# Attention beside an MLP on one core: the output's scale made in the head, other lengths for the pieces of other work, transposes ahead of the lengths

## The chip, the core and the metric

The kernel runs on one core of a Trainium2 chip. Its time is the device time of an execution in microseconds; three runs are given, and their median is the kernel's time. A profiled execution of its own gives the trace.

## What is computed

The input x has 2048 rows of 640. It is normalised by row, and the result xn goes two ways: attention with 32 heads of 20, and an MLP that normalises once more. Both are added to x.

```
xn = layernorm(x)
qkv = (xn @ wqkv) -> q, k, v of 32 heads, 2048 x 20 each
p = softmax(q @ k.T * 20**-0.5)          # 2048 x 2048, 32 times
A = concat(p @ v) @ wo
h = gelu(layernorm(xn) @ w1 + b1)        # 2048 x 1536, tanh form
B = h @ w2 + b2
out = x + A + B
```

## The kernel before

**Number formats.** Most products are of float32 values that are split into a high and a low float16 part, and three matmuls (high by high, high by low, low by high) stand for one. A weight is scaled by a power of two before it is split. `pow2` (line 107) makes that scale from sums of squares: a tiny matmul (tile mxp) adds 128 partitions' sums by a matrix of ones, and VectorE reduces it and takes the exponent with a few one-column operations (`lo_`, `hi_`, `s_` tiles). `scale_of` (456) calls it for q, k, v, w1, w2 and wo, under the tags "q", "k", "v", "1", "2" and "o". The tile of mxp comes from the pool psM (one buffer) for the tags "k" and "o", otherwise from psS (three buffers, which the scores share).

**The head** (up to 183 us). Four chunks of 512 rows of x are normalised (`norm_a`, `norm_b`, `norm_c`), transposed (for chunk 1 by TensorE in `transp`, with `transp_out` to evict), and multiplied with wqkv (`qk`, tiles qkp; `qk_out` evicts to qkhl by ScalarE L367 and VectorE L368; `vproj` and `vproj_all` make the values). `lengths` adds squares of q and k by head on TensorE (tile norms). Five steps a chunk are written out as strings at line 643, one letter per action: "4" and "6" are lengths, "!", "@" and "#" the three transposes of chunk 1, "t" an eviction of one of them, "c" is norm_c, "o" is qk_out, "q" and "y" ask for a piece of w1 and of w2, "w" makes the scale of v, and "s" takes one step of `weights()`, a generator that squares, scales and splits w1 and that collects the squares of wo.

**The loop** (183 to 1265 us) has 64 passes: 16 pairs of heads, two halves of the queries, two quarters in each half. A pass works on 512 queries of two heads in 16 units of 128 keys. For a unit TensorE makes the scores (L786, tile s in one of psS's three buffers), ScalarE the exponential (L788, tile p, seven buffers), and TensorE the product with the values (L818, tile o). In half of the units p is a sum of its upper bfloat16 half and a float16 rest `low`, which VectorE subtracts (L800, four buffers); the products of four units are issued together.

Beside this run the pieces of other work on TensorE: the first layer of the MLP (tile pu, 30 matmuls of 256 columns for one evicted tile), the second layer (py, 36 of 320), the values of the later heads (pz, 15 of 480) and at last the output product (z, 15 of 320). All four share psM's single buffer. A finished pu tile starts a `gelu`, a chain of eight operations on VectorE (L1010 to L1025) with a tanh on ScalarE between (L1021).

The order is by a table. PLAN has seven rows of steps for a pass: "s" is a unit's scores and exponential, "v4" the products of the four oldest units, "l4" the low part of unit 4, "e" the eviction of the pass before, "m" a piece of other work, and "t" or "r" a tick. A tick moves every side job by one step: a gelu, an eviction, the loads of the next heads, the finishing of results, the split of w2 and wo. With "r" a gelu's tanh waits one tick more. RATE gives the three "m" of a pass their lengths in us of TensorE: `other` saves them up as credit and cuts a tile's matmuls at the nearest places. Where a new gelu starts while the one before is unfinished, the rest of the old one is issued first (line 1085).

In pass 4 the generator `values` (1147) takes one "m" for the scales: it makes f2, fills a second ones tile (`wones`, GpSimd), calls `scale_of("o")`, makes fo from it, and starts the split of w2 (`second_split`).

After the loop 27 of the 32 output tiles are left.

Of the kernel before, what the change touches and what calls it, by code (L numbers as in the profile page):

```python
# [9 lines left out]
F32 = mybir.dt.float32  # L10
# [4 lines left out]
ALU = mybir.AluOpType  # L15
# [3 lines left out]
P = 128  # L19
# [13 lines left out]
KROW = 32768.0  # L33
GRP = 4
CHUNK = 2.1
RATE = (1.75, 1.95, 1.9)
PLAN = ('s s t v4 e l0', 's s t s l1 r m r r l4', 's s v4 l5', 's s r t m', 's s s l8 r v4', 's l9 r l12 s l13 m', 's r s v4')
UNITS = (3, 3, 3, 3, 2, 2)
ENDS = tuple(sum(UNITS[: i + 1]) for i in range(len(UNITS)))
TAIL = 12  # L40
# [3 lines left out]
MC = 256  # L44
# [4 lines left out]
def mha_mlp_kernel(tc, x, wqkv, wo, w1, b1, w2, b2, out):  # L49
# [4 lines left out]
    with (  # L54
# [53 lines left out]
        def pow2(acc, tag, total=None):  # L108

            lo = keep.tile([P, 1], F32, name=f"lo_{tag}")  # L110
            hi = keep.tile([P, 1], F32, name=f"hi_{tag}")
            if total is None:
                if tag in "ko":
                    pt = psM.tile([P, 512], F32, tag="m", name="mxp")
                else:
                    pt = psS.tile([P, 2, 512], F32, tag="s", name="mxp")[:, 0, :]
                n = acc.shape[1]
                nc.tensor.matmul(pt[:, :n], ones_of[0], acc, start=True, stop=True)
                nc.vector.tensor_reduce(lo, pt[:, :n], AX.X, ALU.add)  # L119
                total = lo  # L120
            nc.vector.tensor_scalar(lo, total, 2.0**-100, 2.0**120, ALU.max, ALU.min)

            nc.vector.tensor_scalar(lo.bitcast(I32), lo.bitcast(I32), 0x7F000000, 1,
                                    ALU.bitwise_and, ALU.logical_shift_right)
            if tag == "q":

                scales[tag] = keep.tile([P, 1], F32, name=f"s_{tag}")
                nc.vector.tensor_scalar(hi.bitcast(I32), lo.bitcast(I32), 0x3F800000, None, ALU.bitwise_xor)
                nc.vector.tensor_scalar(scales[tag], hi, 2.0**76, None, ALU.mult)
                return lo, hi  # L130
            whole(lo, hi)
            return lo, hi
# [46 lines left out]
        with tc.tile_pool(name="pa", bufs=2) as pa, tc.tile_pool(name="pa1", bufs=1) as pa1, tc.manual_schedule():  # L179
# [278 lines left out]
            def scale_of(tag, total=None):  # L458
                pw[tag] = pow2(accs[tag], tag, total)
                if tag not in scales:  # L460
                    scales[tag] = keep.tile([P, 1], F32, name=f"s_{tag}")
                    nc.vector.tensor_scalar(scales[tag], pw[tag][1], 4096.0, None, ALU.mult)
                if tag == "k":
                    back(tag)
# [37 lines left out]
            def weights():  # L502

                for k in range(KD):
                    if k == 0:
                        accs["1"] = sm.tile([P, 8], F32, tag="acc1", name="acc1", bufs=1)[:, :KD]
                    nc.scalar.activation(junk[:, :F], w1t[:, k, :], AF.Square, accum_out=accs["1"][:, k : k + 1])
                    yield
                scale_of("1")
                yield  # L510
                factors()
                yield

                accs["o"] = sm.tile([P, 8], F32, tag="acco", name="acco", bufs=1)[:, :KD]
                came = []
                for n in range(3 * KD):
                    k, q = divmod(n, 3)
                    if q == 2:
                        nc.scalar.activation(junk[:, :D], came[-1], AF.Square, accum_out=accs["o"][:, k : k + 1])
                    split(pa, w1t[:, k, q * 512 : (q + 1) * 512], w1v[:, k, q, 0], w1v[:, k, q, 1], scales["1"], 512)  # L520
                    if q == 0:
                        came.append(pa.tile([P, D], F32, tag="wtmp", name="wos"))
                        nc.gpsimd.dma_start(came[-1], wo[k * P : (k + 1) * P, :])
                    yield

            def second():

# [92 lines left out]
            for c in range(4):  # L620
                nxt = c + 1 if c < 3 else None
                for tt in range(5):
                    if c == 0 and tt == 1:
                        norm_b2(0)
                        norm_c(0)

                        nc.scalar.activation(junk[:, :1], ones[:, :1], AF.Exp)
                        ps = qk(0, 1, lambda: scale_of("k"))
                        hl = qk_out(0, 0, first)
                        split_qkv("q", c0=4 * P)  # L630
                        split_qkv("k")
                    else:
                        ps = qk(c, tt)
                    if c == 0:
                        if tt == 0:
                            split_qkv("q", c0=2 * P, c1=4 * P)
                            sums("k", [stage["k"][:, 0:3], stage["k"][:, 3:]])
                            first = ps
                            continue
                        elif tt == 1:  # L640
                            qk_sq(0, 0, hl)
                            pts = []
                    for step in (('', 'qvo', 'ao', 'bo', '4q!y@c#otyxttSywz'), ('zos', 'qa6yqoPsbiqs', 'jkso', 'lcsV4o', 'sxoy'), ('ssoa6bzijP', 'yo', 'zs4ossc', 'klozV', 'uozs'), ('so', 'os6', 'oszs', 'ssosPsVfze4', 'o'))[c][tt]:
                        if step == "a":
                            norm_a(nxt)
                        elif step == "b":
                            norm_b(nxt)
                        elif step == "c":
                            norm_c(nxt)
                        elif step in "!@#":  # L650
                            transp(1, 2 * "!@#".index(step), pts)
                        elif step == "t":
                            transp_out(*pts.pop(0))
                        elif step in "46":
                            lengths(int(step))
                        elif step == "x":
                            load_x(c + 2)
                        elif step == "s":
                            some(1)
                        elif step == "q":  # L660
                            ask(1)
                        elif step == "z":
                            next(slices2, None)
                        elif step == "y":
                            next(asked2, None)
                        elif step == "v":
                            sums("v", [stage["v"][:, 0:3], stage["v"][:, 3:]])
                        elif step == "w":
                            scale_of("v")
                            split_qkv("v")  # L670
                        elif step == "u":
                            for s in range(2):
                                nc.sync.dma_start(vwscr[:, :, s], wv[:, :, 2, s, VC:])
                        elif step == "f":
                            factors_out()
                        elif step == "S":
                            qk_sq(0, 4, hl)
                        elif step == "o":
                            hl = qk_out(c, tt, ps)
                        elif step == "P":  # L680
                            vp = vproj(c - 1)
                        elif step == "V":
                            head_values(c - 1, vp)
                        elif step == "e":
                            early = [load_features(mc) for mc in range(2)]
                        else:
                            turn(nxt, "ijkl".index(step))
# [13 lines left out]
            some(99)  # L701
            for _ in slices2:
                pass


        with ExitStack() as scope:
# [438 lines left out]
            def values(hv, feats):  # L1145

                step = (D - VC) / 2400
                for kb in range(NKB - 4):
                    c, j = divmod(kb, MC // P)
                    if kb == 2:  # L1150
                        yield 1, 0.2
                        nc.vector.tensor_scalar(f2, ulo, 2.0**-14, pw["2"][0], ALU.mult, ALU.mult)
                        nc.vector.tensor_scalar(f2, f2, 2.0**-13, None, ALU.mult)
                        ones_of[0] = m1.tile([P, 2 * MC], F32, tag="w", name="wones")[:, :P]
                        nc.gpsimd.memset(ones_of[0], 1.0)
                        scale_of("o")
                        nc.vector.tensor_scalar(fo, pw["v"][0], 2.0**-22, pw["o"][0], ALU.mult, ALU.mult)
                        late.append(second_split())
                        patient.append(late[0])
                        yield 0.2  # L1160
                    yield 3 * KD, 3 * KD * step
                    ps = psM.tile([P, 512], F32, tag="m", name="pz")
                    n = 0
# [313 lines left out]
```

## Time and profile before

| | us |
|---|---|
| three runs | 1326.13, 1329.0, 1329.7 |
| median | 1329.0 |
| the profiled execution | 1328.16 |
| its span, first to last instruction | 1326.3 |
| TensorE (PE) busy | 1314.0 |
| ScalarE (ACT) busy | 1116.3 |
| VectorE (DVE) busy | 1065.3 |
| granted TensorE clock | 0.999 |

The difference of 1.9 us between the execution and its span lies outside the recorded instructions. PE counts as busy while a matmul is issued or under way, so its busy share is not its peak. In the chain of waits and in the timeline a row begins with the start and the length in us; `x15` is a count of merged instructions, and a bracket tells how long the engine idled before and what ended it. In rows of groups there stand, behind the bar, the busy us and the mean ns of one, and behind the second bar the idle time before them.

### The profile page before, as it was taken

How to read it: one execution, taken by the hardware profiler on the slowest of the kernel's cores; microseconds unless marked ns; L12 is line 12 of the kernel's file. 1: busy time of each engine (PE TensorE's matmuls, PEld its weight loads, DVE VectorE, ACT ScalarE, POOL GpSimd, SP SyncE). 2: the span in 40 equal slices, each digit the busy share in tenths (PEclk: the TensorE clock that was granted, in tenths of full speed). 3: DMA queues.
4: the chain of work that ended last, by engine and by line, in shares of the span. 5: the costliest groups of instructions: out<-in, count | busy, mean ns of one | idle time of the engine just before them, and what ended most of it. 6: DMA issues, size and time to landing. Idle time of an engine off the chain costs nothing.

```text
span 1326.3 us, 29078 instructions
## 1 busy us (share of the span) xinstructions
PE 1314.0 (99%) x11636; PEld 604.2 (46%) x11636; DVE 1065.3 (80%) x1450; ACT 1116.3 (84%) x1306; POOL 36.1 (3%) x85
## 2 busy tenths in 40 slices
PE   9999999999999999999999999999999999999998
PEld 6454564333344444444444444444444444443466
DVE  7667569898699887889988798987889898988642
ACT  7745369999999999999999999999999999989900
POOL 2000000000000000000000000000000000000000
PEclk9999999999999999999999999999999999999999
DMA  8697531121233321142312034222124332253266
GB/s 308 215 276 214 190 103 35 39 63 53 77 82 99 86 57 33 44 120 64 97 47 68 17 88 123 69 55 58 50 59 117 92 87 70 71 158 100 87 216 192
DMA packets 108166, 135.28 MB, mean 102 GB/s; under 512 B 24308, under 2 KB 74376, under 8 KB 107900
## 3 DMA queue, kind: packets, MB, share of 16 engines
q1 hardware_dynamic: 104588, 125.99, 31.9%
q0 software_dynamic: 2816, 6.90, 2.7%
q8 instruction: 92, 1.51, 0.5%
q10 hardware_dynamic: 624, 0.51, 0.1%
q14 instruction: 46, 0.38, 0.1%
HBM read 86.64 MB, written 43.74 MB: 98 GB/s over the span
## 4 chain that ended last, share of the span: by engine, by line
PE 72%; DVE 15%; ACT 5%; DMA 4%; issue 2%; SPq 1%; ACTq 0%; DVEq 0%; POOLq 0%
PE o L818 23%; PE s L786 15%; PE pu L1079 10%; PE py L1114 8%; DVE low L800 6%; PE qkp L352 6%; PE z L1264 5%; PE pz L1166 3%; ACT p L788 2%; PE vp L425 1%; DMA xb<-in_B_b_dram 1%; DVE w L1014 1%; DVE u L1012 1%; DVE u L1010 1%; DVE w L1016 1%
## 5 line engine op out<-in xcount | busy, mean ns | idle before, releaser
L788 ACT ACTIVATE p<-s 128x1024 f32<-128x1024 f32 x1024 | 968.7, 1057 | 56.2 <-PE s L786 53.9
L800 DVE TENSOR_TENSOR low<-p 128x1024 f16<-128x1024 f32 x512 | 605.7, 1219 | 72.8 <-ACT p L788 71.4
L818 PE MATMUL o<-p,vfull 128*32 128x512 bf16 (+1 forms) x4096 | 384.1, 493 | 0.0
L786 PE MATMUL s<-qs,ks 61*128 61x512 f16 x2048 | 303.5, 381 | 3.0 <-ACT p L788 2.1
L786 PEld LDWEIGHTS <-ks 61*128 61x128 f16 x2048 | 75.7, 94 | 234.8 <-issue 215.8
L1114 PE MATMUL py<-w2t,hT 128*128 128x320 f16 x1152 | 171.5, 300 | 0.9 <-DVE xb L1041 0.9
L1079 PE MATMUL pu<-xm,w1t 128*128 128x256 f16 x1440 | 171.4, 273 | 0.1
L1079 PEld LDWEIGHTS <-w1t 128*128 128x128 f16 x1440 | 134.3, 98 | 43.9 <-issue 29.3
L818 PEld LDWEIGHTS <-vfull 128*32 128x32 f16 x3072 | 61.1, 95 | 183.3 <-issue 182.7
L1114 PEld LDWEIGHTS <-hT 128*128 128x128 f16 x1152 | 105.6, 98 | 71.2 <-issue 33.9
L352 PE MATMUL qkp<-xnt,wv 128*128 128x512 f16 x600 | 131.4, 379 | 1.6 <-DVE lo L119 0.8
L818 PE MATMUL o<-low,vfull 128*32 128x512 f16 x1024 | 101.5, 378 | 0.1
L352 PEld LDWEIGHTS <-wv 128*128 128x128 f16 x600 | 58.0, 98 | 70.9 <-issue 1.7
L818 PEld LDWEIGHTS o<-p,vfull 128*32 128x32 f32 x2048 | 61.8, 108 | 58.3
L1264 PE MATMUL z<-w1t,ot 128*128 128x320 f16 x480 | 66.7, 299 | 0.0
L1010 DVE TENSOR_TENSOR u<-pu,r2f 128x512 f32<-128x512 f32 x48 | 33.1, 689 | 36.2 <-PE pu L1079 36.0
L1264 PEld LDWEIGHTS <-ot 128*128 128x128 f16 x480 | 46.3, 98 | 21.0 <-issue 3.3
L367 ACT ACTIVATE qkhl<-qkp,qks 128x1024 f16<-128x1024 f32 (+1 forms) x24 | 23.2, 965 | 37.2 <-PE qkp L352 15.3
L1221 DVE SCALAR_TENSOR_TENSOR acc<-z,sc,acc 128x320 f32<-128x320 f32 x32 | 17.6, 550 | 42.0 <-PE z L1264 41.7
L368 DVE SCALAR_TENSOR_TENSOR qkhl<-qkp,qks,qkhl 128x1024 f16<-128x1024 f32 (+1 forms) x24 | 26.5, 1105 | 26.1 <-ACT qkhl L367 26.0
L843 ACT ACTIVATE ev<-o 128x512 f32<-128x512 f32 x64 | 39.5, 617 | 3.0 <-PE o L818 2.8
L1104 POOL DMA_DIRECT2D xb<-in_B_b_dram x16 | 13.7, 857 | 953.7 <-DMA xb<-in_A_x_dram 352.4
(206 smaller groups left out, 735.2 us busy)
## 6 DMA issues: line engine op xcount, KB each, us to landing
qkscr<-qkhl SPq DMA_DIRECT2D x40, 256.0 KB
opart<-ev SPq DMA_DIRECT2D x124, 80.0 KB
ks<-qkscr SPq DMA_DIRECT2D x120, 80.0 KB
xm<-xscr SPq DMA_DIRECT2D x13, 640.0 KB
qs<-qkscr SPq DMA_DIRECT2D x192, 40.0 KB
oa<-opart SPq DMA_DIRECT2D x32, 240.0 KB
xt<-in_A_x_dram SPq DMA_DIRECT2D x16, 320.0 KB
xscr<-xnt SPq DMA_DIRECT2D x4, 1280.0 KB
```

Source lines behind the costliest of these rows:

```text
L352: nc.tensor.matmul(ps[:, i, :], wv[:, k, q, a, mm * P : (mm + 1) * P], xnts[c][:, k, b, :], start=(k + n == 0), stop=(k == KD - 1 and n == 2))
L368: nc.vector.scalar_tensor_tensor(hl[:, 1, i0:i1], ps[:, i0:i1], a, hl[:, 0, i0:i1], ALU.mult, ALU.subtract)
L786: nc.tensor.matmul(ps[:, a, :], ks[64 * a : 64 * a + 61, kb * P : (kb + 1) * P], qs[64 * a : 64 * a + 61, cc * 512 : (cc + 1) * 512], star ...
L788: nc.scalar.activation(pt, ps, AF.Exp, scale=QS)
L800: nc.vector.tensor_sub(low, pt, upper(pt))
L818: nc.tensor.matmul(pv.o[32 * q : 32 * q + 32, :], src[:, v0 - PAD * (1 - q % 2) :][:, :32], t, start=q not in pv.begun, stop=last, skip_gr ...
L843: nc.scalar.activation(evs[g, hf][:, cc], o, AF.Copy)
L1010: nc.vector.tensor_mul(u, ps, r2f[:, None, :].to_broadcast([P, 2, MC]))
L1079: nc.tensor.matmul(ps[:, i], w1v[:, k, (f + i) // 4, a, fo_ : fo_ + P], xnt[:, k, b, :], start=(n == 0), stop=(n == 3 * KD - 1))
L1114: nc.tensor.matmul(ps[:, :320], hTs[mc][:, f, a, j * P : (j + 1) * P], w2v[:, f, b, hf * 320 : (hf + 1) * 320], start=(n == 0), stop=(n == ...
L1166: nc.tensor.matmul(ps[:, : D - VC], feats[c][:, k, a, j * P : (j + 1) * P], hv[:, k, b, :], start=(n == 0), stop=(n == 3 * KD - 1))
L1264: nc.tensor.matmul(ps[:, :320], ot[:, k, a, j * P : (j + 1) * P], wov[:, k, b, h * 320 : (h + 1) * 320], start=(n == 0), stop=(n == 3 * KD ...
```

## The change

Five edits. RATE and PLAN get other numbers and another order. The tag "1" joins those whose mxp tile is of psM. The scale of wo and the factor fo are made as the last step of `weights()`, in the head, and f2 at the head's end; the step in `values` goes, and with it the second ones tile. In the head's strings chunk 0's last step has the transposes first and the lengths behind them, and norm_c behind two evictions.

```
-RATE = (1.75, 1.95, 1.9)
-PLAN = ('s s t v4 e l0', 's s t s l1 r m r r l4', 's s v4 l5', 's s r t m', 's s s l8 r v4', 's l9 r l12 s l13 m', 's r s v4')
+RATE = (2.0, 1.4, 2.2)
+PLAN = ('s s t v4 l0 e', 's s l1 t s r m', 's s t v4', 's s l4 r l5 l8 m', 's s t l9 s r v4', 's l12 s m l13', 's r s v4')
...
-                if tag in "ko":
+                if tag in 'ko1':
...
+                scale_of("o")
+                nc.vector.tensor_scalar(fo, pw["v"][0], 2.0**-22, pw["o"][0], ALU.mult, ALU.mult)
...
-                    for step in (('', 'qvo', 'ao', 'bo', '4q!y@c#otyxttSywz'), ...
+                    for step in (('', 'qvo', 'ao', 'bo', '!y@#4qottctyxSywz'), ...
...
+            nc.vector.tensor_scalar(f2, ulo, 2.0**-14, pw["2"][0], ALU.mult, ALU.mult)
+            nc.vector.tensor_scalar(f2, f2, 2.0**-13, None, ALU.mult)
...
                     if kb == 2:
-                        yield 1, 0.2
-                        nc.vector.tensor_scalar(f2, ulo, 2.0**-14, pw["2"][0], ALU.mult, ALU.mult)
-                        nc.vector.tensor_scalar(f2, f2, 2.0**-13, None, ALU.mult)
-                        ones_of[0] = m1.tile([P, 2 * MC], F32, tag="w", name="wones")[:, :P]
-                        nc.gpsimd.memset(ones_of[0], 1.0)
-                        scale_of("o")
-                        nc.vector.tensor_scalar(fo, pw["v"][0], 2.0**-22, pw["o"][0], ALU.mult, ALU.mult)
                         late.append(second_split())
                         patient.append(late[0])
-                        yield 0.2
```

The lines behind these edits move by two to four: L800 of before is L804 of after, L1010 is L1014.

On VectorE, in the head where the last step of chunk 0 ends, the three bt operations of norm_c (they read what GpSimd made) stood between the two evictions of q and k (qkhl); xnt is the evicted transpose that the next chunk's products read.

```order
 L287 SCALAR_TENSOR_TENSOR ve<-ve,mv 128x4
 L288 TENSOR_SCALAR ve<-ve 128x4
-L368 SCALAR_TENSOR_TENSOR qkhl<-qkp,qks,qkhl 128x1024
+L368 SCALAR_TENSOR_TENSOR qkhl<-qkp,qks,qkhl 128x1024 x2
+L322 TENSOR_TENSOR xnt_587<-pt,xnt_587 128x2x512 x2
 L249 TENSOR_TENSOR bt<-rall 128x4
 L250 SCALAR_TENSOR_TENSOR bt<-ve,bt 128x4
 L251 SCALAR_TENSOR_TENSOR rall<-bt,rall 128x4
-L368 SCALAR_TENSOR_TENSOR qkhl<-qkp,qks,qkhl 128x1024
-L322 TENSOR_TENSOR xnt_605<-pt,xnt_605 128x2x512 x2
-L322 TENSOR_TENSOR xnt_605<-pt_629,xnt_605 128x512
+L322 TENSOR_TENSOR xnt_587<-pt_607,xnt_587 128x512
```

The second qkhl and two of the three xnt now come ahead of the bt operations.

On VectorE in pass 4 of the loop the operations of the scale (lo_o, hi_o, s_o) and of the two factors (sc) stood between low parts; the rows of before there are these.

```order
L800 TENSOR_TENSOR low<-p 128x1024 x2
L1152 TENSOR_SCALAR sc<-lo_u,lo_1634 128x1
L1153 TENSOR_SCALAR sc<-sc 128x1
L119 TENSOR_REDUCE lo_o<-mxp 128x1
L121 TENSOR_SCALAR lo_o<-lo_o 128x1
L123 TENSOR_SCALAR lo_o<-lo_o 128x1
L135 TENSOR_SCALAR lo_o<-lo_o 128x1
L105 TENSOR_SCALAR hi_o<-lo_o 128x1
L462 TENSOR_SCALAR s_o<-hi_o 128x1
L1157 TENSOR_SCALAR sc<-lo_v,lo_o 128x1
L800 TENSOR_TENSOR low<-p 128x1024
```

After the change the same nine stand at the end of the head, between the last split of w1 and the loop's first low parts, and mxp stands on TensorE ahead of the last 30 value products.

On VectorE in the loop, a gelu's chain and the low parts of a pass; first before, in pass 17, where a pass holds one gelu from its start and the next starts at its end.

```order
L1010 TENSOR_TENSOR u<-pu,r2f 128x512
L1012 TENSOR_TENSOR u<-u,b1t 128x512
L1014 TENSOR_TENSOR w<-u 128x512
L1016 SCALAR_TENSOR_TENSOR w<-w,u 128x512
L800 TENSOR_TENSOR low<-p 128x1024 x2
L1023 SCALAR_TENSOR_TENSOR u<-w,u 128x512
L1024 TENSOR_SCALAR hT<-u,sc 128x2x256
L1025 SCALAR_TENSOR_TENSOR hT<-u,sc,hT 128x2x256
L800 TENSOR_TENSOR low<-p 128x1024 x4
L1010 TENSOR_TENSOR u<-pu,r2f 128x512
```

Then after, in pass 31, from the fourth operation of the first gelu on; the last row takes in two low parts of the pass and two of the next.

```order
L1020 SCALAR_TENSOR_TENSOR w<-w,u 128x512
L804 TENSOR_TENSOR low<-p 128x1024 x2
L1027 SCALAR_TENSOR_TENSOR u<-w,u 128x512
L1028 TENSOR_SCALAR hT<-u,sc 128x2x256
L1029 SCALAR_TENSOR_TENSOR hT<-u,sc,hT 128x2x256
L1014 TENSOR_TENSOR u<-pu,r2f 128x512
L1016 TENSOR_TENSOR u<-u,b1t 128x512
L1018 TENSOR_TENSOR w<-u 128x512
L804 TENSOR_TENSOR low<-p 128x1024
L1020 SCALAR_TENSOR_TENSOR w<-w,u 128x512
L804 TENSOR_TENSOR low<-p 128x1024 x4
```

The second gelu now starts right behind the first one's end, with three low parts of the pass still to come. On TensorE, pass 31 of before has the pieces pu15, pu15, pu15 and of after pu15, pu30, py10 (tile and number of matmuls); passes 24, 38, 45 and 52 of after hold the same three. Passes 3 and 5 of after hold 22 and 24 pz matmuls; passes 5 to 8 of before hold 30 each.

2 lines of the change are left out of this document (1 added, 1 removed).

## The prediction

> **What bounds the kernel now.** I read the page first, then busy time by stretch, then the chain of waits, and last the timeline at the places that the change touches. The profiled execution took 1328.16 us with a span of 1326.3 us, so 1.9 us lie outside the span; the median of the three runs is 1329.0 us.
>
> ```profile
> PE 1314.0 (99%) x11636; PEld 604.2 (46%) x11636; DVE 1065.3 (80%) x1450; ACT 1116.3 (84%) x1306; POOL 36.1 (3%) x85
> L788 ACT ACTIVATE p<-s 128x1024 f32<-128x1024 f32 x1024 | 968.7, 1057 | 56.2 <-PE s L786 53.9
> L786 PE MATMUL s<-qs,ks 61*128 61x512 f16 x2048 | 303.5, 381 | 3.0 <-ACT p L788 2.1
> ```
>
> TensorE is busy 99% of the span; ScalarE's exponentials wait 53.9 us for scores, while the scores wait 2.1 us for exponentials. Of the loop the stretches say the same (columns: stretch, its length, then PE, PEld, DVE, ACT; the first row is of the head).
>
> ```profile
> 60.00:90.00 30.00, 29.66 (x215) 15.81 (x213) 18.99 (x43) 17.12 (x26) 3.08 (x3) 1.00 1.00 304
> 210.00:300.00 90.00, 88.48 (x769) 33.42 (x768) 82.27 (x107) 85.56 (x100) 0.20 (x1) 1.00 0.19 53
> 300.00:400.00 100.00, 99.46 (x891) 38.42 (x889) 80.02 (x93) 95.63 (x110) 0.91 (x1) 1.00 0.26 70
> 500.00:600.00 100.00, 99.90 (x953) 43.81 (x949) 81.67 (x95) 94.83 (x109) 1.74 (x2) 1.00 0.23 66
> 1000.00:1100.00 100.00, 99.51 (x942) 44.17 (x943) 90.91 (x116) 93.06 (x106) 1.71 (x2) 1.00 0.35 93
> L843 ACT ACTIVATE ev<-o x64: 597/597/689, 201.2 to 1264.6; 128x512 f32<-128x512 f32 x64
> ```
>
> A busy PE is not yet a PE at its peak, so I checked that its pieces have one pace. These are pieces of the other work in the chain of waits (start, length):
>
> ```profile
> 474.78 1.74 PE pu L1079 x15
> 490.93 2.82 PE py L1114 x20
> 496.48 2.28 PE py L1114 x16
> 528.99 3.38 PE pu L1079 x30
> ```
>
> Fifteen more pu matmuls cost 1.64 us, so 0.109 each and 0.10 us for a piece; four more py cost 0.54, so 0.135 each and 0.12 for a piece. The pieces stretch for nobody. The 64 passes take (1264.6 - 201.2)/63 = 16.88 us each, all of it PE's. Over 210 to 300 PE idles 1.5 us, over 300 to 400 0.5, over 1000 to 1100 0.5: there is little waiting to win.
>
> **The new RATE and PLAN.** RATE adds to 5.6 us a pass before (1.75 + 1.95 + 1.9) and after (2.0 + 1.4 + 2.2). PLAN keeps PE's sequence: 2 scores, products, 3 scores, other work, 2, products, 2, other work, 3, products, 2, other work, 2, products. The rest after the loop is the same, 27 output pieces of 15. So PE's sum stays, but for one piece more (0.10 us). What can change is waiting. Ticks fall from 10 to 8 a pass, and the low parts stand elsewhere on VectorE. I cost this at 0 and bound it on both sides.
>
> Below nothing: PE's idle rows (1.5 + 0.5 + 0.5 above, less the 1.26 priced next) leave some 1.2 us in these 290 us, or some 4 in the 1080 of the loop; that is the bound: -4. Above nothing: five passes (24, 31, 38, 45, 52, counted from 0) now hold pu15, pu30, py10, in which a second gelu begins two ticks after the first and drains it. There VectorE runs, from the first gelu's start to the pass's last low part, 9 operations of 0.69, one of 0.49, one of 0.75, and 6 low parts:
>
> ```profile
> 476.56 0.69 DVE L1010 TENSOR_TENSOR u<-pu,r2f 128x512 f32<-128x512 f32 x1 [0.93 <-PE pu L1079]
> 482.35 0.49 DVE L1024 TENSOR_SCALAR hT<-u,sc 128x512 f16<-128x512 f32 x1
> 482.88 0.75 DVE L1025 SCALAR_TENSOR_TENSOR hT<-u,sc,hT 128x512 f16<-128x512 f32 x1
> 483.55 4.62 DVE L800 TENSOR_TENSOR low<-p 128x1024 f16<-128x1024 f32 x4
> 489.79 0.39 PE L818 MATMUL o<-low,vfull 128*32 128x512 f16 x4
> ```
>
> At 4.62/4 = 1.16 a low part that is 6.21 + 1.24 + 6.93 = 14.4 us. In this pass of before (three pu15, 5.22 us of other work) the chain would run from 476.56 to 490.9; the products that need it start at 489.79, and in the longer pass (1.74 + 3.38 + 1.47 = 6.59) 1.37 later, at 491.16. So 0.2 us of cover are left where before had 489.79 - 488.17 = 1.6. If the cover is gone, each such pass costs what is missing: I bound it by one drained gelu end, 0.69 + 0.49 + 0.75 = 1.93 us, times 5 = +10. I take 0, since at the rows' lengths the chain still fits.
>
> **The scale of the output, in the loop.** Pass 4 spends one of its three pieces on it: PE runs the little product mxp, has nothing to fill with, and runs into the exponentials.
>
> ```profile
> 257.54 0.64 PE L786 MATMUL s<-qs,ks 61*128 61x512 f16 x4
> 258.11 0.39 PE L118 MATMUL mxp<-acco,wones 128*128 128x5 f32 x2
> 258.70 0.39 PE L786 MATMUL s<-qs,ks 61*128 61x512 f16 x2 [0.21 <-ACT p L788]
> 259.62 0.39 PE L786 MATMUL s<-qs,ks 61*128 61x512 f16 x2 [0.53 <-ACT p L788]
> 260.53 0.39 PE L786 MATMUL s<-qs,ks 61*128 61x512 f16 x2 [0.52 <-ACT p L788]
> 260.86 1.50 PE L818 MATMUL o<-p,vfull 128*32 128x512 bf16 x16
> ...
> 532.37 0.75 PE s L786 x6
> 534.77 0.54 PE s L786 x4
> ```
>
> From 257.54 to 260.86 are 3.32 us; the same four and six scores take 0.54 + 0.75 elsewhere. So 2.03 us go (1.26 of it as idle rows), and the piece of other work that was put off is done in either case. What is late next is the exponential itself: passes 3 and 5 of after hold 22 and 24 of the long pz matmuls where passes 5 to 8 of before hold 30, so part of this wait may come back there (a rival below).
>
> **The scale, at the head's end.** mxp now stands before the last 30 value products. On VectorE nine operations of 0.15 to 0.21 us follow, some 1.6 us.
>
> ```profile
> 96.96 0.28 PE L118 MATMUL mxp<-acc,ones 128*128 128x1 f32 x2
> 97.17 0.52 PE L397 MATMUL norms<-sq,heads 128*32 128x128 bf16 x24
> ...
> 170.51 12.40 PE L425 MATMUL vp<-wv,xnt 128*128 128x320 f16 x90
> 182.84 0.61 PE L786 MATMUL s<-qs,ks 61*128 61x512 f16 x4
> 184.59 2.36 DVE L800 TENSOR_TENSOR low<-p 128x1024 f16<-128x1024 f32 x2 [6.58 <-ACT p L788]
> ```
>
> A mxp costs PE 97.17 - 96.96 = 0.21 us: +0.21, as the value products run without a gap up to the first scores. VectorE idles 6.58 us up to 184.59, so from 178.0; mxp runs near 178.7 (two thirds of 170.51 to 182.84), so its nine operations end near 180.5 under that cover, and would cost their 1.6 us only if the first low part came 4 us sooner. GpSimd's memset of the second ones tile (0.2 us) goes from an idle engine: 0.
>
> **Transposes ahead of the lengths.** VectorE's chain sets PE's next start here; the three bt operations, which wait on GpSimd, now stand behind both evictions L368.
>
> ```profile
> 47.68 1.28 DVE L368 SCALAR_TENSOR_TENSOR qkhl<-qkp,qks,qkhl 128x1024 f16<-128x1024 f32 x1
> 48.88 0.15 DVE L249 TENSOR_TENSOR bt<-rall 128x4 f32<-128x4 f32 x1
> 49.38 1.28 DVE L368 SCALAR_TENSOR_TENSOR qkhl<-qkp,qks,qkhl 128x1024 f16<-128x1024 f32 x1
> 50.59 2.94 DVE L322 TENSOR_TENSOR xnt<-pt,xnt 128x1024 f16<-128x1024 f32 x3
> 51.85 13.11 PE L352 MATMUL qkp<-xnt,wv 128*128 128x512 f16 x60 [0.75 <-DVE xnt L322]
> ```
>
> The second L368 can start at 48.96 in place of 49.38: -0.42. PE runs on from 51.85 to 64.96 and idles 0.3 us from 60 to 90 (first row of the stretches above), so I let it last. One w1t load now stands behind a w2t load on SP's queue; the loads after it keep their place, so 0, and up to the whole 0.42 lost if a load ends last. The scale of w1 takes its product from the single psM buffer instead of a psS one: its last reader there is done 18.8 us earlier, so 0.
>
> ```profile
> 70.07 0.48 DVE L401 TENSOR_REDUCE lmx<-norms 128x1 f32<-128x128 f32 x2
> ...
> 89.38 0.28 PE L118 MATMUL mxp<-acc,ones 128*128 128x5 f32 x2
> ```
>
> **Sum.** 1328.16 - 2.03 + 0.10 + 0.21 - 0.42 + 0 = 1326.0 us.
>
> **Rivals.**
> - *The new order also clears other waits* (-4): 1322 us. For it: fewer VectorE operations between low parts. Against: PE idles hardly at all from 500 to 600. Chance 0.27.
> - *VectorE's drained gelus hold the products up*: the chain of 14.4 us above, in passes 24, 31, 38, 45 and 52. With 0.2 us of cover, it decides from some 0.6 us missing a pass, which eats the 2.1 won; at 1.93 it gives 1326.0 + 9.7 = 1336 us. For it: 1000 to 1100 has VectorE at 91%. Against: low parts have 1.6 us of cover elsewhere. Chance 0.13.
> - *The change does not do what it says*: the wait on exponentials moves to passes 3 and 5, and the head's 0.42 ends in a load: 1326.0 + 1.26 + 0.42 = 1327.7 us. Chance 0.16.
> - *ScalarE, not PE, sets the loop*: its 16 x 0.946 + 0.62 + 0.50 = 16.26 us a pass is near 16.88, and if the new order halved the 56.2 us of waiting, 1300 us. The pieces' equal pace speaks against it. The Trainium skill (Perfetto Trace Analysis, Identifying the Most-Contended Engine) says that matmul busy time misjudges TensorE and that weight loads should be read; by it, PEld's 46% leaves room. Here the order of PE's work, not its busy share, is the evidence. Chance 0.02.
> My forecast has the remaining 0.42.
>
> The 0.946 is 968.7/1024; 0.62 and 0.50 are the eviction's and the tanh's rows:
>
> ```profile
> L843 ACT ACTIVATE ev<-o 128x512 f32<-128x512 f32 x64 | 39.5, 617 | 3.0 <-PE o L818 2.8
> L1021 ACT ACTIVATE w<-w 128x512 f32<-128x512 f32 x48 | 32.2, 672 | 0.0
> ```
>
> **The numbers.** A measurement of this kernel tells about 0.3% (4 us) from no change. Faster by more: the first rival and the last, 0.29. Slower by more: the gelus at their worse end, 0.12. Within: 0.59. The range takes in the first rival with its bound (1326.0 - 4, and 2 more as its bound comes from few rows: 1320) and two thirds of the gelus' price (1332).
>
> **What would show it.** Right: no mxp between scores after 190, no idle row on s before 262 of 0.5 us, qkp's 60 matmuls starting near 51.4, first scores near 182.6, last eviction near 1262.5, PE idle below 0.1 us per 100 from 500 on. Wrong: products of low waiting on VectorE at the end of passes 24, 31, 38, 45, 52; scores waiting on exponentials near 235 to 270; last eviction after 1265.

## The result, and the profile after

| | before | after |
|---|---|---|
| median of 11 executions, us | 1328.64 (1326.13 to 1329.7) | 1330.68 (1329.09 to 1334.05) |
| ratio, 95% interval | | 1.0022 [1.0013, 1.0030] |
| profiled execution, its span, us | 1328.16, 1326.3 | 1331.92, 1330.1 |

The change costs 0.22%, some 2.9 us by the ratio (its interval is 1.7 to 4.0 us; the medians lie 2.0 us apart). The forecast was 2.1 us the other way.

The page of the changed kernel looks like that of before; the waits of scores for exponentials fell, as hoped.

```profile
PE 1315.2 (99%) x11636; PEld 603.7 (45%) x11636; DVE 1066.8 (80%) x1450; ACT 1117.1 (84%) x1306; POOL 36.0 (3%) x84
...
L790 PE MATMUL s<-qs,ks 61*128 61x512 f16 x2048 | 304.4, 381 | 1.7 <-ACT p L792 1.1
L352 PE MATMUL qkp<-xnt,wv 128*128 128x512 f16 x600 | 133.1, 382 | 3.9 <-DVE qkhl L368 3.8
```

The last row is the one to stop at: the qkp matmuls of the head wait 3.9 us. Where the time goes is read from the first and the last eviction of the loop, 206.2 and 1268.5 (201.2 and 1264.6 before).

```profile
L847 ACT ACTIVATE ev<-o x64: 597/597/679, 206.2 to 1268.5; 128x512 f32<-128x512 f32 x64
```

So in these two executions the head is 5.0 us longer, the loop 1.1 shorter (1062.3 against 1063.4), and what follows equal (61.6 against 61.7). Of the 5.0, 0.6 lie ahead of the first qkp matmul, which starts at 15.33 instead of 14.72; that start differs from one execution to the next. **The loss is all in the head.** TensorE's rows there, after:

```profile
51.96 13.11 PE L352 MATMUL qkp<-xnt,wv 128*128 128x512 f16 x60
...
83.84 6.65 PE L352 MATMUL qkp<-xnt,wv 128*128 128x512 f16 x30 [0.78 <-DVE qkhl L368]
90.33 0.28 PE L118 MATMUL mxp<-acc,ones 128*128 128x5 f32 x2
93.59 8.32 PE L352 MATMUL qkp<-xnt,wv 128*128 128x512 f16 x30 [2.98 <-DVE qkhl L368]
...
187.77 0.61 PE L790 MATMUL s<-qs,ks 61*128 61x512 f16 x4
```

At 51.96 after is 0.11 behind (51.85 before). Then come a gap of 0.78, one of 2.98, and thirty matmuls that take 8.32 instead of 6.63: the clock fell. Before had here one gap of 0.83 us. Their sum, 0.11 + 0.78 + (2.98 - 0.83) + 1.69, is 4.7 of the 4.9 by which the first scores (the s matmuls) come later (187.77 against 182.84).

The gap names VectorE's eviction, which waits for ScalarE's, and ScalarE waits for loads. First SyncE's queue near 50 to 60, before and then after (start, length of the issue):

```profile
50.47 1.24 SPq L373 DMA_DIRECT2D qkscr<-qkhl  x2
51.76 0.93 SPq L539 DMA_DIRECT2D w2t<-in_B_w_dram  x1
52.78 2.79 SPq L197 DMA_DIRECT2D xt<-in_A_x_dram  x4
56.92 0.54 SPq L324 DMA_DIRECT2D xscr<-xnt  x1
```

```profile
51.15 1.34 SPq L373 DMA_DIRECT2D qkscr<-qkhl  x2
54.14 0.54 SPq L324 DMA_DIRECT2D xscr<-xnt  x1
54.73 1.21 SPq L541 DMA_DIRECT2D w2t<-in_B_w_dram  x1
56.04 4.57 SPq L197 DMA_DIRECT2D xt<-in_A_x_dram  x4
```

Before, the second w2t load and the four x loads are asked for and only then the store of the transposes (xscr), which waits for their last eviction. After, the store stands ahead of them, and the load goes out 3.0 us later. ScalarE's rows that read these loads and the qkp evictions behind them, before and then after:

```profile
59.85 1.27 ACT L530 ACTIVATE junk<-w2t 128x1280 bf16<-128x1280 f32 x1 [0.32 <-DMA w2t<-in_B_w_dram]
...
61.12 1.09 ACT L367 ACTIVATE qkhl<-qkp,qks 128x1024 f16<-128x1024 f32 x1
...
84.01 1.48 ACT L507 ACTIVATE junk<-w1t 128x1536 bf16<-128x1536 f32 x1 [0.97 <-DMA w1t<-in_B_w_dram]
...
87.31 1.12 ACT L367 ACTIVATE qkhl<-qkp,qks 128x1024 f16<-128x1024 f32 x1
```

```profile
64.17 1.27 ACT L532 ACTIVATE junk<-w2t 128x1280 bf16<-128x1280 f32 x1 [4.06 <-DMA w2t<-in_B_w_dram]
...
65.44 1.09 ACT L367 ACTIVATE qkhl<-qkp,qks 128x1024 f16<-128x1024 f32 x1
...
87.76 1.48 ACT L507 ACTIVATE junk<-w1t 128x1536 bf16<-128x1536 f32 x1 [2.77 <-DMA w1t<-in_B_w_dram]
...
91.06 2.12 ACT L367 ACTIVATE qkhl<-qkp,qks 128x1024 f16<-128x1024 f32 x2
```

ScalarE idles 4.06 us for a load that it needs there only for a sum of squares (the output junk is not used), and the eviction behind it is 4.3 us late. TensorE has work in hand there and doesn't feel it, but all that follows in this chain is 1.5 to 4 us late, a w1t load with it, for whose squares ScalarE waits again (2.77), and here TensorE has no work left.

### The profile page after: what moved, and what is told of

Read it like the earlier page. It is cut to its first block, busy times and chain, and to the rows that moved or that the text cites. A ratio compares the mean times of both kernels' runs of the same rounds, so it can differ in the third digit from the quotient of the medians.

```text
span 1330.1 us, 29050 instructions
## 1 busy us (share of the span) xinstructions
PE 1315.2 (99%) x11636; PEld 603.7 (45%) x11636; DVE 1066.8 (80%) x1450; ACT 1117.1 (84%) x1306; POOL 36.0 (3%) x84
## 4 chain that ended last, share of the span: by engine, by line
PE 90%; ACT 3%; DVE 3%; DMA 2%; issue 1%; SPq 0%; ACTq 0%; DVEq 0%
PE o L822 31%; PE s L790 20%; PE py L1118 12%; PE pu L1083 12%; PE qkp L352 5%; PE z L1260 5%; PE pz L1162 2%; ACT p L792 1%; PE vp L425 1%; PE vp L446 1%; DVE qkhl L368 1%; ACT wv L476 1%; DMA xt<-in_A_x_dram 1%; DMA w1t<-in_B_w_dram 1%; ACT junk L101 0%
## 5 line engine op out<-in xcount | busy, mean ns | idle before, releaser
L804 DVE TENSOR_TENSOR low<-p 128x1024 f16<-128x1024 f32 x512 | 610.5, 1220 | 122.9 <-ACT p L792 121.9
L1162 PE MATMUL pz<-hv,xm 128*128 128x480 f16 x180 | 39.9, 367 | 0.0
```

The lines of the kernel that those rows point to most:

```text
L804: nc.vector.tensor_sub(low, pt, upper(pt))
L1162: nc.tensor.matmul(ps[:, : D - VC], feats[c][:, k, a, j * P : (j + 1) * P], hv[:, k, b, :], start=(n == 0), stop=(n == 3 * KD - 1))
```

## The experiments

My theory (A) was that SyncE's queue did it, through ScalarE. The rivals: (B) the new psM buffer for w1's scale, (C) chance in one profiled execution, (D) the transposes ahead of the lengths themselves. For the loop, a second pair of theories stands with the runs. The rounds are 7 to 12 executions of each kernel beside executions of before. The table gives for each kernel the rounds' median in us and its ratio to before on the same chip with a 95% interval, and from its profiled execution the time from the first qkp matmul to the first scores ("head"; the start of the first qkp matmul differs between executions, from 14.6 to 16.7 us), the gap ahead of the thirty qkp matmuls near 90 to 95, and the time from the first to the last eviction ("loop"). Of thirteen intervals, one that only just leaves 1 out is weak evidence by itself.

| kernel | median | ratio | head | gap | loop |
|---|---|---|---|---|---|
| before | 1328.64 | | 168.12 | 0.83 | 1063.40 |
| after | 1330.68 | 1.0022 [1.0013, 1.0030] | 172.44 | 2.98 | 1062.27 |
| after again | 1331.10 | 1.0016 [1.0005, 1.0027] | 173.22 | 3.38 | 1062.20 |
| before + new order in the head | 1330.39 | 1.0026 [1.0009, 1.0043] | 170.24 | 1.94 | 1061.64 |
| before + psM for w1's scale | 1327.62 | 0.9994 [0.9984, 1.0003] | 167.79 | 0.49 | 1061.78 |
| before + scale in the head | 1332.11 | 1.0027 [1.0017, 1.0037] | 168.98 | 1.55 | 1066.67 |
| before + RATE and PLAN | 1329.15 | 1.0010 [1.0000, 1.0021] | 168.17 | 0.88 | 1062.99 |
| after, old order in the head | 1327.88 | 0.9997 [0.9987, 1.0006] | 167.38 | none | 1062.37 |
| after, w2t load ahead | 1326.85 | 0.9989 [0.9980, 0.9998] | 168.57 | 1.66 | 1062.65 |
| after, psS for w1's scale | 1330.59 | 1.0016 [1.0004, 1.0027] | 170.36 | 2.19 | 1062.59 |
| after, squares behind the eviction | 1327.48 | 0.9992 [0.9982, 1.0002] | 168.72 | 1.80 | 1064.51 |
| after, w2t and w1t loads ahead | 1325.52 | 0.9980 [0.9970, 0.9989] | 166.78 | none | 1060.78 |
| before + scale in the head, empty ticks | 1329.09 | 0.9997 [0.9988, 1.0006] | 168.95 | 1.54 | 1063.94 |
| before, w1t load ahead | 1326.95 | 0.9990 [0.9981, 0.9999] | 167.14 | none | 1062.83 |

**The parts alone, added to before.** The new order in the head:

```
-(... '4q!y@c#otyxttSywz')
+(... '!y@#4qottctyxSywz')
```

> The kernel before with one edit: the new order of steps in the head (transposes ahead of the lengths), and nothing else. Theory A (the queue): the second w2t load now stands on SyncE's queue behind the xscr store, which waits for the last evicted transpose; ScalarE's squares of w2t wait for it some 4 us near 60 to 64, the qkp eviction stands behind them, and TensorE pays between 82 and 102. It expects the whole loss of the head here: first scores near 187.8 (182.8 before), a gap in TensorE of about 3 us near 93, then 30 qkp matmuls in 8.3 us instead of 6.6, and 1328.6 + 4.9 = 1333.5 us. Theory B (the buffer): the loss comes from the product of w1's scale, which no longer takes a psS buffer; it expects no loss here: first scores near 182.8, 1328.6 us. Theory C (chance): transfers were slow in one profiled execution; first scores within 0.5 of 182.8, and no difference in the rounds.

Measured: 1.0026, as large a loss as the changed kernel's. The squares of w2t wait as in the changed kernel and the stall is there, though shorter than expected and with no slow matmuls behind it:

```profile
90.70 0.39 PE L118 MATMUL mxp<-acc,ones 128*128 128x5 f32 x2 [0.42 <-ACT vfull L614]
93.02 6.63 PE L352 MATMUL qkp<-xnt,wv 128*128 128x512 f16 x30 [1.94 <-DVE qkhl L368]
...
185.38 0.60 PE L786 MATMUL s<-qs,ks 61*128 61x512 f16 x4
```

First scores at 185.38, not 187.8: B and C fall, and A had the place right, but its size too large: 1330.39 us, where it expected 1333.5. The psM buffer:

```
-                if tag in "ko":
+                if tag in 'ko1':
```

> The kernel before with one edit: the product of w1's scale takes the psM buffer. Theory A: no loss; the qkp matmuls after it need no longer wait for the product to be read, so the 0.83 us gap at 90.48 shrinks to the wait for the eviction, some 0.7 us: first scores near 182.2, 1328.6 - 0.7 = 1327.9 us. Theory B: the loss of the head is here: a gap of about 3 us near 90, first scores near 187.8, 1333.5 us. Theory C: 1328.6 us, nothing either way.

Measured: 0.9994, and first scores at 182.53. B falls; the gain of 0.3 in the head is what the gap lost (0.49 for 0.83), and within what executions differ by. The scale in the head, with all else of before:

```
+                scale_of("o")
...
                     if kb == 2:
-                        yield 1, 0.2
...
-                        yield 0.2
```

The first line stands at the end of `weights()`, followed by fo, and f2 is made at the head's end, as in the change.

> The kernel before with one edit: the output's scale and f2 are made at the head's end, and pass 4 no longer holds them (with the old plan, the old order of steps and the old buffer). All theories of the head expect the head's end to cost 0.2 us (one more product on TensorE): first scores near 183.0. The forecast's term for the loop says that 2.0 us go: 1328.6 + 0.2 - 2.0 = 1326.8 us, last eviction near 1262.8 (1264.6 before). The rival: the wait on exponentials moves to other passes, since the long pz pieces come earlier: the loop loses 0.8 only (2.03 less the 1.26 of idle rows), 1328.0 us, last eviction near 1264.0.

Measured: 1.0027, slower by 3.6 us where both theories had it faster or level. The first row below is the loop's first five intervals between evictions, the second the other 58, first of before and then of this kernel (stretch, length, then PE, PEld, DVE, ACT):

```profile
201.24:287.83 86.59, 85.07 (x759) 34.16 (x757) 79.81 (x103) 81.92 (x97) 0.20 (x1) 1.00 0.13 36
287.83:1264.64 976.81, 974.22 (x9091) 419.49 (x9088) 828.06 (x997) 917.58 (x1035) 15.14 (x18) 1.00 0.28 78
```

```profile
202.08:287.11 85.03, 84.58 (x757) 33.79 (x755) 77.68 (x93) 81.62 (x96) 0.00 (x0) 1.00 0.13 37
287.11:1268.75 981.64, 978.16 (x9091) 420.78 (x9088) 829.20 (x998) 917.51 (x1035) 15.46 (x18) 1.00 0.28 77
```

The first five give back 1.56 of the 2.03 that the forecast priced. Then, with the same 9091 matmuls, the rest takes 4.8 us more. What it is shows in places like this one (VectorE and TensorE, near 376 us):

```profile
375.94 0.75 DVE L1029 SCALAR_TENSOR_TENSOR hT<-u,sc,hT 128x512 f16<-128x512 f32 x1
...
376.61 3.49 DVE L804 TENSOR_TENSOR low<-p 128x1024 f16<-128x1024 f32 x3
...
377.88 0.40 PE L822 MATMUL o<-low,vfull 128*32 128x512 f16 x3 [0.32 <-DVE low L804]
```

A gelu's last operations stand ahead of the pass's last three low parts, and TensorE waits for these. It is the mechanism of the second rival of the forecast, though not with the new plan but with the old one. Most of it isn't shown as idle time: PE is "busy" 978.16 against 974.22 us with as many matmuls. Of the 3.9 us between, 3.0 are in the products of low parts, which count as busy for 95.0 us in these 58 intervals against 92.0 before. RATE and PLAN alone:

```
-RATE = (1.75, 1.95, 1.9)
+RATE = (2.0, 1.4, 2.2)
...
```

> The kernel before with one edit: the new RATE and PLAN. After's loop is 1.1 us shorter than before's between the first eviction and the last, and the forecast gave 1.9, so 0.8 are missing. Theory P: the plan costs them: 1328.6 + 0.8 = 1329.4 us, last eviction near 1265.4. Theory Q: the plan costs nothing and the scale gives less than the 2.0: 1328.6 us, last eviction near 1264.6. First scores near 182.8 by both.

Measured: 1.0010 with an interval that begins at no change; loop 1062.99. Between P and Q the loop's length alone doesn't decide: before's own loop lasted 1061.64 to 1063.40 in four profiled executions. What makes these differ is in the last section, and with it the profiles lean to P.

**One thing undone in the changed kernel.** The old order in the head, all else of the change kept:

```
-(... '!y@#4qottctyxSywz')
+(... '4q!y@c#otyxttSywz')
```

> The changed kernel with one edit undone: the old order of steps in the head. Theory A (the queue): the w2t load goes early again, the head is before's with the psM buffer (some -0.3) and one more product (+0.2): first scores near 182.8, the changed kernel's loop of 1062.3 us behind it, 1330.7 - 5 = 1325.7 us. Theory B (other parts of the change make the head longer): first scores above 185, 1329 us or more.

Measured: 0.9997, first scores at 182.54, no gap, last eviction 1263.35. The place is as A had it; its time of 1325.7 us was missed by 2.2, since the 5 us taken off came from one profile, while the rounds put the loss at 2 to 3. The other four edits together change nothing that the rounds can tell. Now only the load, with the new order kept:

```
-(... '!y@#4qottctyxSywz')
+(... '!y@#4qyottctxSywz')
```

> The changed kernel with one step moved: the second w2t load is asked for right behind the w1t load, ahead of the qkscr store and the last transposes' store; the new order of transposes and lengths stays. Theory A (the queue): the load is issued near 51, ScalarE's second squares of w2t start near 60 instead of 64.2, no gap of TensorE over 1 us between 82 and 102, first scores near 182.5, 1325.5 us. Rival D (the transposes ahead of the lengths cost the time on VectorE and ScalarE themselves, not by the queue): the squares come early but first scores stay above 185, 1328.5 us or more.

Measured: 0.9989; against the changed kernel's 1.0022 that is some 4 us, nearly all that A expected. The squares come at once, and a gap stays, for the other load (ScalarE, then TensorE):

```profile
59.45 1.27 ACT L532 ACTIVATE junk<-w2t 128x1280 bf16<-128x1280 f32 x1
...
84.81 1.48 ACT L507 ACTIVATE junk<-w1t 128x1536 bf16<-128x1536 f32 x1 [2.50 <-DMA w1t<-in_B_w_dram]
```

```profile
50.40 0.41 PE L397 MATMUL norms<-sq,heads 128*32 128x128 bf16 x16
...
51.25 13.11 PE L352 MATMUL qkp<-xnt,wv 128*128 128x512 f16 x60
...
90.71 6.63 PE L352 MATMUL qkp<-xnt,wv 128*128 128x512 f16 x30 [1.66 <-DVE qkhl L368]
```

D falls, as the transposes still precede the lengths. First scores came at 183.21 and not at 182.5, and the gap is above the 1 us that A allowed, since A had not priced the w1t load. Next, the buffer undone:

```
-                if tag in 'ko1':
+                if tag in "ko":
```

> The changed kernel with one edit undone: the product of w1's scale takes a psS buffer again. Theory A with the clock: the stall stays, but the product now stands between its two halves as in the run with the new order of steps alone (0.42 + 1.94 us in place of one gap of 2.98), TensorE's clock is granted in full after it, and 30 qkp matmuls take 6.6 us instead of 8.3: first scores near 185.6, 1330.7 - 2.2 = 1328.5 us. Rival: the slow 8.3 us came by chance or with the whole stall; first scores within 0.5 of 187.8 or of 185.6 without the buffer deciding it, and the rounds show no difference from the changed kernel (1330.7 us).

Measured: its profiled execution came out as A had it (mxp at 90.46, thirty qkp matmuls in 6.63, first scores 185.54), and the rounds gave 1.0016, as the changed kernel. So the 2.2 us that A gave the buffer are not seen in the rounds; how often the slow stretch comes in executions that aren't profiled stays open. Then the squares behind the eviction, with the loads left late:

```
-('zos', 'qa6yqoPsbiqs', ...
+('osz', 'qa6yqoPsbiqs', ...
```

> The changed kernel with one step moved behind another: in the step after the transposes the squares of w2t (and of w1t) come behind the qkp eviction on ScalarE instead of ahead of it; the loads stand where the change put them. Theory A, in its second half (the late load does harm because ScalarE executes in order and the eviction stands behind the wait): the eviction starts near 61 instead of 65.4, TensorE's gaps between 82 and 102 fall below 1.5 us in all, first scores near 183.5, 1326.5 us. Rival E (the x loads, also behind the store, are what is late): the eviction is early, but the norms' statistics and the transposes stay 2.5 us late and first scores stay above 185, 1328.5 us or more.

Here "z" takes the squares of w2t and "o" evicts. Measured: 0.9992. The eviction no longer waits, though the load does come late:

```profile
61.07 1.09 ACT L367 ACTIVATE qkhl<-qkp,qks 128x1024 f16<-128x1024 f32 x1
...
65.48 1.27 ACT L532 ACTIVATE junk<-w2t 128x1280 bf16<-128x1280 f32 x1 [1.85 <-DMA w2t<-in_B_w_dram]
```

Its first scores, at 185.1, would speak for E, but that execution began its first qkp matmul at 16.38 instead of 14.72; the head itself took 168.72, and the rounds agree with A. What E says should be late isn't: from the first qkp matmul to ScalarE's first row of the next chunk (L333) are 58.9 us, 58.8 before and 60.7 in the changed kernel. The gap of 1.80 is above the 1.5 that A allowed; ScalarE still waits 2.71 us for the w1t load there. So this late load does next to no harm by itself: it costs because ScalarE works in order and the eviction stands behind the wait. This and the run before it are why the rounds, not one profile, carry the verdicts here.

**Again, and further.** The changed kernel once more:

> The changed kernel once more, beside the others: 1.0022 of before, 1331.5 us. It tells whether the slow stretch behind the stall (30 qkp matmuls in 8.3 us) belongs to the changed kernel. If it does, it is there again, first scores near 187.8; if it came by chance, the same stall is followed by 6.6 us, first scores near 186.

Measured: 1.0016, a gap of 3.38 and the slow 8.32 again. C falls for good. Both loads ahead:

```
-(... '!y@#4qottctyxSywz'), ('zos', 'qa6yqoPsbiqs', ...
+(... '!y@#4qyottctxSywz'), ('zos', 'qa6yqqoPsbis', ...
```

> The changed kernel with two loads asked for earlier: the second w2t load ahead of the store, as in the run with that step alone, and the last w1t load of the step after the next ahead of the qkscr stores instead of right ahead of the squares that read it. Theory A, carried further (any load that ScalarE's in-order queue reads right behind its request puts its landing time into TensorE's path): ScalarE's 2.50 us wait for w1t near 84.8 goes, the evictions behind it start near 85, the gap of 1.66 us before the qkp matmuls at 90.7 goes, first scores near 181.5, 1326.85 - 1.6 = 1325.2 us. Rival: the transposes between (6.6 us on the queue) hold the values' evictions as well, and the gap stays above 1 us: 1326.8 us.

Measured: 0.9980, the only version clearly ahead of before, by 2.7 us, and 5 to 6 ahead of the changed kernel on the medians, as A had it. TensorE is busy without a break from 60 to 120 us:

```profile
60.00:90.00 30.00, 30.00 (x218) 15.96 (x216) 19.54 (x45) 17.18 (x27) 3.09 (x3) 1.00 1.00 316
90.00:120.00 30.00, 30.00 (x218) 16.21 (x217) 23.66 (x68) 12.87 (x21) 2.90 (x3) 1.00 0.78 236
```

Its head is 1.34 us shorter than before's. Of the 2.6 us by which its profiled loop is shorter, 0.95 are a wait for xb that before had in its profile and this one did not (below). For the loop, the scale in the head with the two ticks left empty:

```
                     if kb == 2:
+                        yield 1, 0.2
                         late.append(second_split())
                         patient.append(late[0])
+                        yield 0.2
```

> As the run with the scale alone moved to the head's end, but the two ticks that it took in pass 4 stay in the loop with nothing in them. Theory P (the phase: the loop got 3.3 us longer since all pieces behind pass 4 moved up by a tick and gelus now end beside the pass's last low parts): the pieces keep their places, the waits on low parts go, the wait on exponentials near 260 stays; loop between first and last eviction near 1063.2 (1063.4 before, 1066.7 with the scale alone), 1328.6 us. Theory F (something else that the move brought, such as the missing second tile of ones or VectorE's operations at the loop's start): loop near 1066.7, 1332 us.

Measured: 0.9997, loop 1063.94. The 58 later intervals are back to before's, against 981.64 without the ticks:

```profile
201.95:290.12 88.17, 86.33 (x757) 33.84 (x755) 78.73 (x94) 82.02 (x97) 0.00 (x0) 0.98 0.13 35
290.12:1265.89 975.77, 973.48 (x9091) 419.23 (x9088) 827.69 (x997) 917.47 (x1035) 15.24 (x18) 1.00 0.28 78
```

P is shown: the scale's two ticks held the pieces behind them in the places to which the old plan was fitted; taking them out moved every later piece. (The first five are 1.6 longer than before's as the clock fell there, see the last section.) At last the kernel before with the w1t load ahead:

```
-('zos', 'qa6yqoPsbiqs', ...
+('zos', 'qa6yqqoPsbis', ...
```

> The kernel before with one edit: the last w1t load is asked for ahead of the qkscr stores. By theory A the kernel before already pays for it: ScalarE's wait of 0.97 us near 84 goes and the gap of 0.83 us at 90.5 shrinks; since the product of w1's scale still takes a psS buffer, some 0.3 to 0.6 us of it stay. First scores near 182.4, 1328.2 us; no difference that the rounds can tell.

Measured: 0.9990, some 1.3 us, more than expected: the gap went altogether, so the psS buffer by itself makes none. It hangs on the landing of the w1t load, which is why it lies anywhere from nothing to 1.55 in the kernels of the table with the old order. Whether the buffer adds to it when the load is late isn't separated.

```profile
89.96 0.28 PE L118 MATMUL mxp<-acc,ones 128*128 128x5 f32 x2
90.10 6.63 PE L352 MATMUL qkp<-xnt,wv 128*128 128x512 f16 x30
```

Nothing was run that separates the x loads, which the change moved behind the store too, from the w2t load; moving the w2t load alone left little to find (VectorE waits 0.39 us for an x load there).

## Where the prediction was right and wrong

- **The step that failed**: "One w1t load now stands behind a w2t load on SP's queue; the loads after it keep their place, so 0, and up to the whole 0.42 lost if a load ends last." They don't keep it. The string `!y@#4qottctyxSywz` moved the two steps behind which the store of the transposes becomes due ("t", "t") ahead of "y" and "x", so one w2t load and four x loads now stand behind a store that waits for the last evicted transpose, and go out 3 us later. The working followed the first "q" and "y" of the string and not its second half, nor the queue as a whole. The bound failed too: it took 0.42 as all that could be lost, since that was the gain; what stood behind the load on ScalarE was worth 4.3 us at the eviction and 2 to 5 at TensorE.
- **Transposes ahead of the lengths, -0.42**: right by itself. From the start of transposes and lengths to the next qkp before took 51.85 - 47.43 = 4.42 us (norms of x16 began at 47.43), the changed kernel 51.96 - 47.94 = 4.02. It is the late loads that ate it.
- **The psM buffer, 0**: right, 0.9994 with an interval around 1.
- **The scale at the head's end, +0.21**: right; the product cost 183.60 - 183.46 = 0.14, and VectorE's nine operations ended 4.21 us before the first low part:

```profile
185.16 0.15 DVE L707 TENSOR_SCALAR sc<-sc 128x1 f32<-128x1 f32 x1
189.53 2.36 DVE L804 TENSOR_TENSOR low<-p 128x1024 f16<-128x1024 f32 x2 [4.21 <-ACT p L792]
```

- **The scale out of the loop, -2.03, and RATE and PLAN, 0**: right in place, wrong as two terms that add. With the old plan the scale gave 1.56 back in the first five intervals and then lost 4.8 by the shift of the pieces; with the new plan that loss isn't there (976.64 for the 58 intervals in the changed kernel). As the loops stand, the two are worth about nothing together: 1060.78 to 1064.51 us in seven profiled executions (the changed kernel twice, and its five variants; middle one 1062.37), against 1061.64 to 1063.40 in four (the kernel before, and the three with an edit in the head alone). But a wait for the tile xb lies in these times (last section). Without it, and without 1.67 us of slow matmuls behind it in one of the seven, the seven took 1060.7 to 1060.9 and the four 1061.4 to 1062.5, so a gain of about 1 us is there, and the wait, longer in six of the seven, takes it back. The new plan alone had no such wait and took 1062.99: by these profiles it costs about 1 us, which the forecast put at nothing, and taking the scale out is worth 2.2 under it. The one execution of the new plan alone makes these last two figures estimates. The bound of -4 to +10 was taken for the plan on its own, and the combination stayed within it.
- **The rivals**: none was the case as a whole. The third had half of the truth: the head's 0.42 did end in a load, but its price for that was 0.42, where the head lost 2 to 5 us, and the wait on exponentials did not move to passes 3 and 5 (0.2 us there). ScalarE did not set the loop. VectorE's drained gelus held no product up in the changed kernel, but did so with the old plan once the scale was gone.
- **The signs**: no mxp after 190, no wait of 0.5 us on scores before 262 (0.2 in all, 1.4 before), both right; TensorE's idle time right on the whole from 600 to 1000 (399.68 busy of 400, though 0.27 of the rest lie between 800 and 900) and wrong behind it (265.65 of 268); qkp's sixty matmuls near 51.4, first scores near 182.6 and last eviction near 1262.5, wrong, by 0.6, 5.2 and 6.0 (the first only because this execution's first qkp matmul began 0.61 later), and "last eviction after 1265" was the sign given for a wrong forecast.

## What to carry to other kernels

When a step is moved in a hand-written order, write out each in-order queue that it passes, the issuing queue among them, and ask of each wait what stands behind it: here a store that waits went ahead of a load, the load's reader stood ahead of an eviction, and TensorE paid 30 us later. A load asked for right ahead of its reader on an engine that also evicts is a stall in waiting; asked for some 12 us earlier, it was worth 1.3 us in the kernel before. In a schedule written as a table, taking a step out shifts all that follows, so its price cannot be read from the step's own rows.

## What the runs showed of the hardware

**The clock can fall after short gaps.** In the changed kernel TensorE's granted clock (the column ahead of the DMA share) fell after the gap of 2.98 us, and not in the variant where a product of 0.39 us came just ahead of a gap of 2.19; after and then the variant:

```profile
90.00:94.00 4.00, 1.02 (x7) 0.60 (x5) 2.12 (x3) 2.98 (x7) 0.00 (x0) 1.00 0.76 181
94.00:99.00 5.00, 5.00 (x17) 1.95 (x16) 3.44 (x15) 0.72 (x1) 0.00 (x0) 0.66 0.89 297
```

```profile
90.00:93.00 3.00, 0.67 (x4) 0.30 (x2) 1.55 (x2) 2.71 (x6) 0.00 (x0) 1.00 0.85 164
93.00:99.00 6.00, 5.96 (x28) 2.75 (x29) 3.67 (x15) 0.74 (x2) 0.00 (x0) 1.00 0.82 265
```

The price was 8.32 - 6.63 = 1.69 us on top of the gap. The length of one gap doesn't decide it: a gap of 2.09 us was followed by a clock of 0.63 over 4.6 us (the wait for xb in the run with the squares late, below), and in the kernel with empty ticks three gaps of 0.52 us within 3.5 us (TensorE busy 1.93 of them) brought the clock to 0.67 and 0.50 for the next 3.5 us.

```profile
258.00:261.50 3.50, 1.93 (x18) 0.49 (x10) 2.76 (x4) 3.50 (x5) 0.00 (x0) 1.00 0.72 214
261.50:263.50 2.00, 2.00 (x19) 0.54 (x20) 1.97 (x4) 2.00 (x3) 0.00 (x0) 0.67 0.29 79
263.50:265.00 1.50, 1.50 (x12) 0.13 (x4) 1.50 (x2) 0.68 (x2) 0.00 (x0) 0.50 0.00 0
```

In the kernel before, where the product mxp fills part of the first of these gaps (0.21, 0.53 and 0.52 us; TensorE busy 2.24 of 3.5), the clock stayed at 1.00.

The Trainium skill (TensorE: Matmul & The Clock Gate, Why this matters for your kernels) advises no gaps of TensorE over some 3 us; the gaps of 2.98 and 3.38 agree, the one of 2.09 and the three of 0.52 are below it. The same page of the Trainium skill (What's actually happening) has a window of 3.4 us that runs freely, which would let the place of a gap count as well as its length; no run here tests it.

**A load's landing varied by 2 us.** The w1t load of which the gap hung was asked for at 78.87 before and 80.33 after, and its reader could start at 84.01 and 87.76: 5.1 and 7.4 us later. The changed order alone doesn't explain this: with the old order the same time was 5.1 to 5.6 us in three kernels (before, before with psM, the changed kernel with the old order) and 6.6 to 7.1 in three others (RATE and PLAN, the scale in the head with and without ticks), and 6.9 to 7.4 in the six with the new order that ask for this load as late. So some of the 2.15 us by which the gap grew between the two profiles compared above may be this spread. What decides it isn't settled; asked for earlier, it doesn't matter.

**One wait in the loop differs from one execution to the next.** Near 1190 a piece py waits for xb, the rows of x to which a DMA adds b2; here the changed kernel, and then the run with the squares late, where the matmuls behind the wait are slow as well (4.55 us instead of 2.88):

```profile
1193.06 2.88 PE L1118 MATMUL py<-w2t,hT 128*128 128x320 f16 x20 [1.51 <-DVE xb L1045]
```

```profile
1190.96 4.55 PE L1118 MATMUL py<-w2t,hT 128*128 128x320 f16 x20 [2.09 <-DVE xb L1045]
```

The wait was 0.95 us before and 0 to 0.7 in its three variants with an edit in the head alone, and 1.5 to 2.1 in the changed kernel and its variants, but for the fastest, which had none. With the slow matmuls it makes nearly all of the difference between the loops of the changed kernel and its variants, and somewhat less than half of that between before's. Why it is longer in most of the changed kernels isn't settled.
